# Rotary attention and a SiLU feed-forward on one core: a 128-row step in the products with v, the weights' sign on ScalarE, and a rewritten issue table

## The chip, the core and the metric

The kernel runs on one core of a Trainium2 chip. The metric is the device time of one execution in microseconds (us). The core's engines are TensorE (PE; its weight loads are listed as PEld), VectorE (DVE), ScalarE (ACT), GpSimd (POOL) and SyncE (SP), which here only issues DMAs. Each engine works its own instructions in the order in which they were issued and meets the others at semaphores.

## The reference

```python
# batch 4, heads 8, sequence 576, head size 64; model 512, d_ff 2048
q_rot, k_rot = rotate(q), rotate(k)                 # rotary embedding, halves of 32
scores = q_rot @ k_rot.T / sqrt(64)
attn = exp(scores - max(scores)); attn = attn / (sum(attn) + 1e-9)
x = (attn @ v).transpose(0, 2, 1, 3).reshape(2304, 512)
h = x @ w_in
return (h / (1 + exp(-h))) @ w_out                  # w_in, w_out arrive as float64
```

## The kernel before

Every float32 operand of a product is carried as two float16 parts, hi and lo, with a power-of-two scale that is taken from a norm of the data on the chip. A product is hi\*hi + hi\*lo + lo\*hi, summed in PSUM. Tokens of a batch are numbered in nine blocks of 64.

The work is cut into some 2,700 parts, each with the engines it may run on. The table `ORDER` lists part numbers with a letter for the engine (t TensorE, d VectorE, D VectorE with the sign change fused into the maximum, a ScalarE, p GpSimd, s and A the DMA queues of SP and ACT); a loop at the end issues them in that order. Nothing else sets the order on an engine.

- Attention: 144 slots. A slot has one score product `s` (L798), a row maximum (`max`: fused, L814, or plain, L819, which then needs a separate `neg`), `exp` on ScalarE (L830), a reciprocal of the row sum (`nr0`, `nr1`), then the split of the normalised row: `hi` through `part_hi` (L329 on VectorE or GpSimd, L335 on ScalarE) and `lo` through `part_lo` (one instruction on VectorE, L341; two on GpSimd, L329 and L344). A DMA transpose puts the two halves into `pt`. There are three `e` buffers, three `pn` buffers and two score buffers in PSUM.
- Products with v (`fpv`, L896): 32 groups (8 units by 4 head pairs). Each group has 14 steps over the 9 blocks of `pt`, and each step is two matmuls, one for each head of the pair, into the two halves of the PSUM partitions. In one of the 14 steps (the low part of v, block 4) only 64 of the 128 rows are used.
- Feed-forward: steps of 256 tokens by 256 of d_ff, `m1` (L950), tanh, `g` (L966), again a split `gh`, `gl`, and `m2` (L1006). Unit 0 is streamed while weights arrive; a last unit `rem` holds the remainders of all batches.
- Weights: the float64 bits of 8 pieces of w_in and w_out become float32 in four passes, `wT` (L659), `wC` (L666), `wS` (the sign bit, L675) and `wX` (L683), then a norm, then the split. They come in 12 whole places (1024 values a partition) and 8 half places (512).
- q, k and v: rope in three passes (L479, L483, L486), norms, splits (`qhi`, `qlo`, `vhi`, `vlo`).

Of the kernel before, what the change touches and what calls it, by code (L numbers as in the profile page):

```python
# [9 lines left out]
F16 = mybir.dt.float16  # L10
# [12 lines left out]
# Where the raw weights of a piece's two matrices are put (whole, or two halves): a, b, c are the  # L23
# ring's parts, i / o and a number the split weights' space of a piece that is written later.
# [19 lines left out]
765D 105d 559d 86a 758a 109t 143d 572s 759d 760d 136d 766a 92a 47d 767a 144d 117p 773t 774d 145d 61A 87d 137a
782t 768a 570d 48d 88s 108d 761a 769d 783D 563a 770a 784a 110d 775d 591s 564a 146d 138d 762d 785a 776a 565d 71d
93d 566d 573a 571d 574a 575d 771d 577t 560a 576d 561d 791t 123p 786a 787d 579t 111t 580d 112d 763s 593a 777a
592a 778d 596s 578d 792D 793a 788a 581t 582d 583d 772s 794a 795a 113d 800t 744d 613s 114d 796d 118p 584d 119d
598a 585a 139d 94s 801D 802a 95A 809t 810D 789d 594d 147s 811a 790s 645s 779a 780d 120a 781s 121d 618s 124p 125p
126a 587a 797a 798d 799s 803a 804a 595d 588d 818t 819D 115d 820a 812a 615a 813a 814d 805d 836t 837D 586d 127d
597a 821a 845t 599d 806a 838d 807d 646a 635s 156p 614a 122s 815a 816d 808s 589a 839a 817s 616d 840a 647a 600d  # L50
162p 841d 827t 822a 823d 620a 116d 824a 828D 829d 830a 831a 846d 825d 617d 648d 590d 847a 848a 649d 619a 636a
637a 621d 854t 855d 128s 849d 842p 832d 129A 2051t 638d 843d 856a 833a 834d 149a 826s 2052d 857a 858d 148a 2053d
157p 859d 850d 851a 872t 873D 863t 150t 864D 865d 844s 151d 866a 640s 2054t 163p 152d 164d 860a 874a 852d 639d
867a 835s 875a 641a 861d 868d 642a 890t 891D 643p 881t 882D 869a 892a 893a 883a 870d 894a 876a 853s 603t 2055a
862s 895d 622d 644d 884a 871s 601t 625t 896a 623t 604d 602d 605t 2056d 877d 885a 154d 606d 878a 626d 886d 607d
624d 887a 608d 611a 153d 650t 178s 651d 609a 879d 880s 888d 165a 652t 653d 612d 897p 2057t 2058a 654t 610d 655d
627t 628d 656d 917t 629d 155d 657d 158p 662a 2059d 630d 918D 919a 899t 900D 901d 660a 658p 166d 659d 920a 921a
902a 898s 908t 922d 903a 909d 631a 904d 935t 936d 923a 924d 663d 910a 889s 905a 686s 193p 937a 632d 911a 912a
2060t 2061a 938a 939a 925s 913d 2062d 926t 927d 944t 945D 946d 914a 664s 688a 928a 906d 907s 633p 634d 2147t
687a 915d 929a 2148a 947a 669s 930a 666a 745d 2149d 2150a 159p 948a 160d 689d 953t 661d 665a 940d 2151d 962t  # L60
# [146 lines left out]
def rope_attention_silu_ffn(  # L207
# [23 lines left out]
    B, H, S, D = q.shape  # L231
# [3 lines left out]
    NR = S // 64  # L235
# [135 lines left out]
    place = {}  # L371
# [737 lines left out]
```

## Time and profile before

| | |
|---|---|
| device time, median of 3 runs | 690.22 us (688.02 to 692.25) |
| span of the profiled execution, first to last instruction | 687.2 us |
| median minus that span | 3.0 us |
| busy share PE / DVE / ACT / POOL | 85% / 79% / 60% / 38% |
| instructions on DVE / ACT / POOL | 1222 / 852 / 217 |

The page lists one profiled execution, of which it gives the span. What lies around the span is the difference to the runs, 0.8 to 5.0 us. Busy time is the union of an engine's instructions. PE is pipelined, so its matmuls overlap, and how densely they are streamed is read from the distance between starts.

### The profile page before, as it was taken

What the parts mean: (1) busy time and instruction counts of PE and PEld (TensorE: products, weight loads), DVE (VectorE), ACT (ScalarE), POOL (GpSimd) and SP (SyncE); (2) the same over time, 40 slices, a digit from 0 to 9 for tenths busy, and PEclk for the clock granted to TensorE, in tenths of its full rate; (3) what the DMA queues carried; (4) which work ended last, traced back from release to release, by engine and by line L of the source; (5) the groups of instructions that cost most, each with busy time, mean ns of one, the idle gap of its engine ahead of it and who ended that gap; (6) DMA issues with size and microseconds to landing.
All of it is one profiled execution on the core that took longest, in us unless ns stands there. A gap on an engine that the chain in (4) does not pass through costs nothing.

```text
span 687.2 us, 12512 instructions
## 1 busy us (share of the span) xinstructions
PE 587.4 (85%) x4428; PEld 375.3 (55%) x4428; DVE 545.2 (79%) x1222; ACT 410.3 (60%) x852; POOL 257.7 (38%) x217
## 2 busy tenths in 40 slices
PE   3534376888799989998699899999999999999997
PEld 2412154645456555655366556656666665666664
DVE  5999989998999899989988989989868787312222
ACT  2488767978797666765455667566765544221421
POOL 1350344224455445342426436344163646022020
PEclk9955567989899999999899999999999999999999
DMA  9999995979699958989567779977964575410201
GB/s 259 236 242 233 275 168 124 237 155 219 128 162 161 188 96 168 173 165 178 97 135 157 135 127 192 164 137 134 197 118 71 104 128 94 54 31 1 47 1 31
DMA packets 233326, 98.33 MB, mean 143 GB/s; under 512 B 214192, under 2 KB 214448, under 8 KB 233264
## 3 DMA queue, kind: packets, MB, share of 16 engines
q1 hardware_dynamic: 232144, 95.47, 70.3%
q10 hardware_dynamic: 1120, 2.07, 1.5%
q8 instruction: 35, 0.57, 0.4%
q14 instruction: 27, 0.22, 0.1%
HBM read 36.16 MB, written 4.72 MB: 59 GB/s over the span
## 4 chain that ended last, share of the span: by engine, by line
PE 42%; DVE 25%; DMA 16%; ACT 7%; issue 6%; SPq 3%; POOL 1%; ACTq 0%; DVEq 0%; POOLq 0%
PE m L1006 15%; PE m L950 15%; DVE pn L341 6%; DMA pt<-pn 6%; PE pv L896 5%; DVE s L814 4%; PE s L798 3%; DMA w_in<-in_moe_w_in_dram 2%; DVE g L966 2%; DMA io<-in_k_dram 2%; ACT e L830 2%; PE s L354 2%; DMA io<-in_v_dram 2%; DVE vl L341 2%; DMA w_out<-in_v_dram 1%
## 5 line engine op out<-in xcount | busy, mean ns | idle before, releaser
L950 PEld LDWEIGHTS <-w_in 128*128 128x128 f16 x1728 | 167.0, 98 | 35.3 <-issue 5.4
L950 PE MATMUL m<-xh,w_in 128*128 128x256 f16 x1024 | 178.7, 273 | 3.1 <-DVE g L966 3.1
L1006 PE MATMUL m<-w_out,gh 128*128 128x512 f16 x576 | 172.4, 381 | 0.9 <-DVE ob L1019 0.6
L830 ACT ACTIVATE e<-s,small 128x576 f32<-128x576 f32 x144 | 109.7, 762 | 53.4 <-DVE s L814 22.4
L950 PE MATMUL m<-xl,w_in 128*128 128x256 f16 x512 | 139.7, 273 | 0.0
L341 DVE SCALAR_TENSOR_TENSOR pn<-e,small,pn 128x576 f16<-128x576 f32 x123 | 120.3, 986 | 10.9 <-ACT pn L335 5.4
L798 PE MATMUL s<-Tk,Tq 128*128 128x512 f16 (+1 forms) x512 | 90.7, 309 | 36.2 <-ACT e L830 26.8
L1006 PE MATMUL m<-w_out,gl 128*128 128x512 f16 x288 | 109.7, 381 | 2.2 <-DVE gl L341 2.2
L966 DVE SCALAR_TENSOR_TENSOR g<-g,m 128x512 f32<-128x512 f32 x72 | 49.0, 681 | 68.9 <-ACT g L962 43.8
L335 ACT ACTIVATE pn<-e,small 128x576 f16<-128x576 f32 x84 | 64.1, 768 | 45.2 <-DVE small L844 25.6
L814 DVE TENSOR_SCALAR_CACHE_REDUCE s<-s,small 128x576 f32<-128x576 f32 x101 | 81.7, 815 | 9.6 <-PE s L798 9.5
L798 PEld LDWEIGHTS <-Tq 128*128 128x128 f16 x512 | 41.3, 105 | 76.6 <-issue 41.0
L1006 PEld LDWEIGHTS <-gh 128*128 128x128 f16 x576 | 52.4, 100 | 55.5 <-issue 5.5
L962 ACT ACTIVATE g<-m,small 128x512 f32<-128x512 f32 x64 | 43.6, 682 | 61.3 <-PE m L950 56.7
L896 PE MATMUL pv<-pt,vh 128*64 128x256 f16 (+1 forms) x576 | 69.6, 308 | 3.9 <-DMA pt<-pn 1.7
L329 POOL TENSOR_SCALAR pn<-e,small 128x576 f16<-128x576 f32 x39 | 36.7, 941 | 91.2 <-DVE small L844 40.8
L341 DVE SCALAR_TENSOR_TENSOR gl<-g,small,gh 128x512 f16<-128x512 f32 x57 | 47.8, 839 | 10.5 <-ACT gh L335 6.6
L479 POOL TENSOR_TENSOR rt<-io,sin_t 128x576 f32<-128x576 f32 x21 | 32.3, 1547 | 45.8 <-DMA io<-in_k_dram 36.9
L1006 PEld LDWEIGHTS <-gl 128*128 128x128 f16 x288 | 28.2, 98 | 38.7 <-DVE gl L341 5.1
L896 PE MATMUL pv<-pt,vl 128*64 128x256 f16 (+3 forms) x320 | 47.7, 314 | 0.0
L896 PEld LDWEIGHTS <-vh 128*64 128x64 f16 x576 | 34.0, 116 | 20.5 <-issue 10.5
L335 ACT ACTIVATE gh<-g,small 128x512 f16<-128x512 f32 x43 | 30.8, 716 | 15.5 <-DVE g L966 15.2
(144 smaller groups left out, 879.3 us busy)
## 6 DMA issues: line engine op xcount, KB each, us to landing
out_dram<-ob SPq DMA_DIRECT2D x36, 128.0 KB, 2.4
w_in<-in_moe_w_in_dram SPq DMA_DIRECT2D x4, 1024.0 KB, 7.4
w_out<-in_moe_w_out_dram SPq DMA_DIRECT2D x4, 1024.0 KB, 7.3
io<-in_v_dram SPq DMA_DIRECT2D x13, 288.0 KB, 3.9
io<-in_q_dram SPq DMA_DIRECT2D x13, 288.0 KB, 3.3
io<-in_k_dram SPq DMA_DIRECT2D x13, 288.0 KB, 3.7
io<-in_v_dram SPq DMA_DIRECT2D x13, 256.0 KB, 4.5
ring<-in_moe_w_in_dram SPq DMA_DIRECT2D x3, 1024.0 KB, 6.0
```

The lines of the kernel that those rows point to most:

```text
L329: e.tensor_scalar(out=out, in0=in0, scalar1=s1, scalar2=s2, op0=ALU.mult, op1=ALU.bypass if s2 is None else ALU.mult)
L335: act.activation(hi, src, AF.Copy, scale=s)
L341: dve.scalar_tensor_tensor(out=lo, in0=src, scalar=s, in1=hi, op0=ALU.mult, op1=ALU.subtract)
L479: eng[e].tensor_tensor(out=buf("rt", b, p, nm), in0=x4()[:, :, ::-1, :], in1=sin_t, op=ALU.mult)
L798: pe.matmul(o, tq[:, j, 2 * c:2 * c + 2, :], kt[:, r0:r1, js], start=(n == 0), stop=(n == 1))
L814: dve.tensor_scalar(out=t, in0=t, scalar1=cc[:, 1:2], scalar2=None, op0=ALU.mult, op1=ALU.min, accum_out=m_of(1, 2),)
L830: act.activation(buf("e", i), buf("s", i)[:, 0:S], AF.Exp, bias=m_of(1, 2), scale=-1.0 if fused[i] else cc[:, 0:1], accum_out=m_of(2, 3),)
L896: pe.matmul(o[64 * j:64 * j + 64, 0:m], vt[part][0:k, j, s, :], pt[0:k, a, j, 0:m], start=(z == 0), stop=(z == len(steps) - 1),)
L950: pe.matmul(t[:, c, 0:n], w[:, wz, kk, fs], xx[:, kk, 0:n], start=(kk == 0 and x == 0), stop=(kk == KD - 1 and x == 2),)
L962: act.activation(g[:, :, 0:n], t[:, :, 0:n], AF.Tanh, scale=th_v[units[u][0]][:, i:i + 1])
L966: dve.scalar_tensor_tensor(out=g, in0=g, scalar=1.0, in1=t, op0=ALU.add, op1=ALU.mult)
L1006: pe.matmul(o, gs[gz][:, c, ts], w[:, wz, c], start=(first and c == 0 and x == 0), stop=(last and c == 1 and x == 2),)
```

## The change

It has three pieces.

1. In `fpv` every step uses all 128 rows. In the one step that used 64, the other 64 rows hold the low part of the first block on both sides, so the product gains one lo\*lo term.
2. `wS` may run on ScalarE, as one activation that writes float16.
3. `ORDER` is another table: the same 2,691 parts, in another order, and many of them on other engines. RAW_PLACE, GROUPS, the buffers and all other functions are as they were.

```diff
@@ fS
-                    if se == "d":
+                    if se == "a":
+                        act.activation(tu[:, :, 1].bitcast(F16), tf[:, :, 1], AF.Copy, scale=2.0 ** 30)
+                    elif se == "d":
                         dve.tensor_scalar(
                             out=tu[:, :, 1], in0=tu[:, :, 3], scalar1=0x8000, scalar2=None, op0=ALU.bitwise_and
                         )
...
-                n3 = add("wS", key, "dp", fS, [n1, n2], tb, it)
+                n3 = add("wS", key, "adp", fS, [n1, n2], tb, it)
@@ fpv
             for z, (a, part, s) in enumerate(steps):
-                k = 64 if part == "l" and a == 4 else 128
                 for j in range(2):
                     pe.matmul(
-                        o[64 * j:64 * j + 64, 0:m], vt[part][0:k, j, s, :], pt[0:k, a, j, 0:m],
+                        o[64 * j:64 * j + 64, 0:m], vt[part][:, j, s, :], pt[:, a, j, 0:m],
                         start=(z == 0), stop=(z == len(steps) - 1),
                     )
@@ ORDER
-4s 0d 5t 3s 1s 6d 21d 15d 7t 2s 38s 41t 22d 23d 8d 39t 42d 16p 540s 40d 9t 10d 11d 62s 12d 24a 13d 63t 43t 17d
...
```

What the new table does to the engines, counted from the built programs (instructions by line, before and after):

| | VectorE | ScalarE | GpSimd |
|---|---|---|---|
| lo halves (`lo` 22, `qlo` 4, `gl` 4 move) | 258 to 228 (L341) | | 42 to 72 (L344) |
| hi halves of rows and of g (`hi`, `gh`) | 39 to 30 | 127 to 103 | 50 to 83 |
| sign of weights | 19 to 1 | 0 to 19 | 1 to 0 |
| row maximum, fused / plain | 101 / 43 to 84 / 60 | | |
| rope passes | 33 to 49 | | 63 to 47 |
| v hi, x hi, outputs | 16 to 27 | 52 to 39 | 2 to 4 |
| `wT` and `wC` | 0 to 4 | 40 to 34 | 0 to 2 |
| `neg` and `nr0` instructions | 64 to 77 | 123 to 127 | |

Three of the 16 `ksw` parts (two DMAs each) also go from the ACT queue to the SP queue. On TensorE the parts stand almost as they did: counted in TensorE work, the first `m1` and each unit's steps stand where they stood.

VectorE near its start, before. `w_in` and `w_out` are here both the first weight piece (128x1024) and q and k of batch 0 (128x576), which lie in the same space; L479, L483 and L486 are rope passes, L358 reads a norm from PSUM:

```order
L675 TENSOR_SCALAR w_in<-w_in 128x1024
L358 SCALAR_TENSOR_TENSOR junk_128,small<-m_188,id_t 128x128
L486 TENSOR_TENSOR w_out<-w_out,rt 128x576
L310 TENSOR_SCALAR small<-m_160 128x2
L483 TENSOR_TENSOR w_out<-w_out,cos_t 128x576
L329 TENSOR_SCALAR small<-small 128x1
L310 TENSOR_SCALAR small<-m_188 128x1
L486 TENSOR_TENSOR w_out<-w_out,rt 128x576
L316 TENSOR_SCALAR small<-small 128x1
L683 SCALAR_TENSOR_TENSOR w_in<-w_in 128x1024
L341 SCALAR_TENSOR_TENSOR n<-w_in,small,n 128x9x64
L675 TENSOR_SCALAR w_out<-w_out 128x1024
```

VectorE at the same place now (`wX` is L686 in the new file):

```order
L358 SCALAR_TENSOR_TENSOR junk_128,small<-m_204,id_t 128x128
L310 TENSOR_SCALAR small<-m_169 128x2
L316 TENSOR_SCALAR small<-small 128x2
L686 SCALAR_TENSOR_TENSOR w_in<-w_in 128x1024
L329 TENSOR_SCALAR small<-small 128x1
L341 SCALAR_TENSOR_TENSOR n<-w_in,small,n 128x9x64
L358 SCALAR_TENSOR_TENSOR junk_127,small<-m_227,id_t 128x128
L341 SCALAR_TENSOR_TENSOR n<-w_in,small,n 128x9x64
L310 TENSOR_SCALAR small<-m_227 128x1
L486 TENSOR_TENSOR w_out<-w_out,rt 128x576
L316 TENSOR_SCALAR small<-small 128x1
L686 SCALAR_TENSOR_TENSOR w_out<-w_out 128x1024
```

The two sign passes are gone from VectorE. They stand on ScalarE, whose first rows were these before:

```order
L335 ACT_TABLE_LOAD
L335 ACTIVATE n<-w_in,small 128x9x64
L659 ACTIVATE w_in<-w_in 128x1024
L666 ACTIVATE w_in<-w_in 128x1024
L659 ACTIVATE w_out<-w_out 128x1024
L335 ACTIVATE n<-w_in,small 128x9x64
L666 ACTIVATE w_out<-w_out 128x1024
```

ScalarE's first rows now (L676 is the new sign pass):

```order
L659 ACT_TABLE_LOAD
L659 ACTIVATE w_in<-w_in 128x1024
L666 ACTIVATE w_in<-w_in 128x1024
L676 ACTIVATE w_in<-w_in 128x1024
L335 ACTIVATE n<-w_in,small 128x9x64
L659 ACTIVATE w_out<-w_out 128x1024
L666 ACTIVATE w_out<-w_out 128x1024
L676 ACTIVATE w_out<-w_out 128x1024
```

Each weight place now has three passes in a row on ScalarE, and one of the two early q and k halves (`n`) has left it.

GpSimd between the score products of slots 108 and 114, before (`n`, `io` and `rt` belong to q and k of the last batch, `pn` and `e` to attention slots, `gh` to the feed-forward):

```order
L329 TENSOR_SCALAR n<-io,small 128x9x64
L486 TENSOR_TENSOR io<-io,rt 128x576
L329 TENSOR_SCALAR pn<-e,small 128x576
L329 TENSOR_SCALAR gh<-g,small 128x512
L329 TENSOR_SCALAR pn<-e,small 128x576
L329 TENSOR_SCALAR e<-e,small 128x576
L344 TENSOR_TENSOR pn<-e,pn 128x576
L479 TENSOR_TENSOR rt<-io,sin_t 128x576
L483 TENSOR_TENSOR io<-io,cos_t 128x576
L486 TENSOR_TENSOR io<-io,rt 128x576
```

GpSimd between the same two products now:

```order
L329 TENSOR_SCALAR pn<-e,small 128x576
L329 TENSOR_SCALAR gh<-g,small 128x512
L329 TENSOR_SCALAR g<-g,small 128x512
L344 TENSOR_TENSOR gl<-g,gh 128x512
L329 TENSOR_SCALAR gh<-g,small 128x512
L329 TENSOR_SCALAR pn<-e,small 128x576 x2
L479 TENSOR_TENSOR rt<-io,sin_t 128x576
L329 TENSOR_SCALAR pn<-e,small 128x576
L486 TENSOR_TENSOR io<-io,rt 128x576 x2
```

Rope passes have left GpSimd, and halves of slots and of the feed-forward have come in their place.

## Rows read from the trace of the kernel before

**Rows 1.** The page: the span, then busy time, share and instructions of each engine.

```profile
span 687.2 us, 12512 instructions
PE 587.4 (85%) x4428; PEld 375.3 (55%) x4428; DVE 545.2 (79%) x1222; ACT 410.3 (60%) x852; POOL 257.7 (38%) x217
```

**Rows 2.** Busy time by stage: window, length, PE, PEld, DVE, ACT, POOL, clock, DMA.

```profile
20.00:160.00 140.00, 87.01 (x594) 55.91 (x595) 132.77 (x298) 107.38 (x192) 48.98 (x30) 0.72 0.97 207
160.00:500.00 340.00, 313.03 (x2432) 197.36 (x2431) 308.95 (x691) 225.85 (x492) 148.63 (x123) 0.98 0.82 155
500.00:600.00 100.00, 99.00 (x814) 63.41 (x813) 69.47 (x172) 49.71 (x114) 43.78 (x45) 1.00 0.55 95
600.00:687.00 87.00, 82.24 (x559) 54.39 (x556) 20.94 (x32) 22.87 (x52) 14.34 (x16) 1.00 0.10 22
```

**Rows 3.** Groups by form on VectorE: busy us, mean ns of one, idle before.

```profile
L341 DVE SCALAR_TENSOR_TENSOR pn<-e,small,pn 128x576 f16<-128x576 f32 x123 | 120.3, 986 | 10.9 <-ACT pn L335 5.4 <-POOL pn L329 3.6 <-POOL g L329 0.9
L814 DVE TENSOR_SCALAR_CACHE_REDUCE s<-s,small 128x576 f32<-128x576 f32 x101 | 81.7, 815 | 9.6 <-PE s L798 9.5
L819 DVE TENSOR_REDUCE small<-s 128x1 f32<-128x576 f32 x43 | 32.1, 748 | 2.0 <-PE s L798 1.7 <-PE s L804 0.2
L341 DVE SCALAR_TENSOR_TENSOR vl<-io,small,vh 128x320 f16<-128x320 f32 x26 | 20.3, 797 | 3.5 <-ACT vh L335 2.8 <-POOL vh L329 0.7
L814 DVE DVE_READ_ACCUMULATOR s<-s,small 128x1 f32 x101 | 14.1, 139 | 0.0
L329 DVE TENSOR_SCALAR pn<-e,small 128x576 f16<-128x576 f32 x21 | 13.0, 618 | 2.9 <-DMA pt<-pn 2.3 <-DVE small L844 0.4
L483 DVE TENSOR_TENSOR io<-io,cos_t 128x576 f32<-128x576 f32 x7 | 7.6, 1085 | 0.7 <-ACT n L454 0.6
L675 DVE TENSOR_SCALAR w_out<-w_out 128x1024 uint16<-128x1024 uint16 x4 | 5.3, 1325 | 0.2 <-ACT w_out L666 0.2
L675 DVE TENSOR_SCALAR w_in<-w_in 128x512 uint16<-128x512 uint16 x3 | 2.3, 754 | 0.4 <-ACT w_in L659 0.4
```

**Rows 4.** Groups by form on GpSimd.

```profile
L329 POOL TENSOR_SCALAR pn<-e,small 128x576 f16<-128x576 f32 x39 | 36.7, 941 | 91.2 <-DVE small L844 40.8 <-DMA pt<-pn 13.0 <-DVE w_in L683 9.5
L483 POOL TENSOR_TENSOR io<-io,cos_t 128x576 f32<-128x576 f32 x19 | 32.3, 1711 | 20.2 <-ACT small L837 12.8 <-ACT n L454 4.8 <-issue 1.8
L344 POOL TENSOR_TENSOR pn<-e,pn 128x576 f16<-128x576 f32 x21 | 28.6, 1361 | 1.8
L329 POOL TENSOR_SCALAR e<-e,small 128x576 f32<-128x576 f32 x21 | 18.6, 886 | 46.5 <-ACT pn L335 24.7 <-DVE pn L329 11.3 <-ACT small L837 6.0
```

**Rows 5.** A weight pass on ScalarE, by form.

```profile
L659 ACT ACTIVATE w_in<-w_in 128x1024 f32<-128x1024 f32 x4 | 4.5, 1131 | 0.0
```

**Rows 6.** Timeline of VectorE and GpSimd, 206 to 230: start, us, instruction.

```profile
206.53 1.00 DVE L341 SCALAR_TENSOR_TENSOR vl<-io,small,vh 128x320 f16<-128x320 f32 x2
225.31 0.80 DVE L341 SCALAR_TENSOR_TENSOR pn<-e,small,pn 128x576 f16<-128x576 f32 x1
227.92 2.02 DVE L341 SCALAR_TENSOR_TENSOR vl<-io,small,vh 128x320 f16<-128x320 f32 x2
...
227.54 1.59 POOL L344 TENSOR_TENSOR pn<-e,pn 128x576 f16<-128x576 f32 x1
```

**Rows 7.** Timeline of TensorE inside one product with v.

```profile
311.91 0.33 PE L896 MATMUL pv<-pt,vl 128*64 128x320 f16 x2
312.05 0.33 PE L896 MATMUL pv<-pt,vh 128*64 128x320 f16 x2
312.31 0.32 PE L896 MATMUL pv<-pt,vl 64*64 64x320 f16 x2
312.56 0.73 PE L896 MATMUL pv<-pt,vh 128*64 128x320 f16 x8
```

**Rows 8.** The products with v alone by stage: busy TensorE, clock, DMA.

```profile
500.00:687.00 187.00, 18.01 (x228) 1.00 0.34 61
```

**Rows 9.** Shares of the chain that ended last, 0 to 130.

```profile
by line: DMA w_in<-in_moe_w_in_dram 9.5%; DMA io<-in_v_dram 8.0%; DMA w_out<-in_v_dram 7.9%; issue 7.2%; DMA io<-in_k_dram 6.2%; SPq L509 5.5%; PE pv L896 4.8%; DMA Tq<-w_out 4.5%; DVE pn L341 4.0%; PE s L354 4.0%; DVE s L814 3.7%; DMA io<-
```

More of the change, by code (lines that the diff above doesn't have):

```diff
@@ L44 @@
[L44 to L48, printed above, removed]
@@ new lines @@
+1108d 203d 185d 204d 205d 186d 1095d 206a 2072t 2203d 223s 1109a 207d 2204p 208d 242a 1124t 217d 1110d 231s
+2073a 1116D 1125D 1117a 1118a 249p 2205t 2074d 1126d 1101d 1111d 230s 747d 241a 2211t 250p 1112a 1096s 251p
+2206d 1102d 1113d 2208t 2212a 1103a 2213d 1133t 1119a 255d 2214a 243t 2218t 1104d 1127a 2215d 232a 1105s 244d
+1128d 245d 1134d 1114s 246d 1142t 256d 2219a 2216t 252a 247d 2209d 257p 1135a 1120d 2220d 2217t 1129d 253d 2221a
+258p 1136a 2225t 254s 2222p 259d 1121a 1143d 262s 1122d 1144a 1137a 1151t 2226a 1130p 233t 1138d 1152d 1145a
@@ new lines @@
+368a 2335d 369d 2336t 370d 2339a 1419d 394a 409s 2340d 1448t 2337t 1469a 2341d 1420s 1449d 2342p 1436a 402t
+1450d 1451a 2345t 385s 403d 1452a 1470a 1471d 418p 1437d 1411s 404t 2346a 1472p 2343t 405d 411a 1473p 395t 410a
+2344t 396d 406d 1453d 2347d 1484t 2348a 424p 1474s 1457t 2352t 1458d 1454p 1438s 397d 1459a 1485D 1455p 2349d
+1486a 1487a 412t 2353a 1493t 413d 398d 1488d 407d 1460a 2350t 2354d 1456s 414d 1494D 1461a 2355p 392A 1475t
+1462d 425d 1495d 2351t 1463p 1496a 408d 2356d 1497a 399p 1502t 1489d 416d 1490a 2359t 1464d 415d 1503D 1465s
@@ new lines @@
+1880t 1866d 2500t 1881d 1861s 1872d 1882a 1883a 2496d 1867d 1873a 2497d 1868p 1884a 1898t 2501a 2492t 1899D
+1874a 1869d 2498t 1885d 531d 1870s 1886a 2128d 1900a 1901a 1875d 1907t 1876d 2502d 1877p 2129t 1887d 2503a 1878p
+1908d 1889t 1888s 2130d 1909a 2499t 1910a 1890D 2504p 2131d 1879s 1891a 1892a 1902d 1916t 1911d 1903d 1912d
+2132t 1893a 1917d 1918a 1904p 1925t 1913p 2133d 2505t 2134d 1894d 1905d 1926d 2511t 1906s 1919a 1895d 1896p
+2508t 2512a 1914p 1897s 2513d 1943t 2514a 2518t 1944D 1920d 1927d 1945a 1946a 1915s 2506d 1928a 2515d 1921d
@@ new lines @@
+1947a 1952t 1922d 2519a 1979t 1923p 2509a 2520d 2516t 1929a 1930d 1980D 1931a 2525t 1981d 2521p 1924s 1982a
+2522d 1948d 1953D 1949p 1988t 1954a 2526a 1950d 2517t 1932d 1951s 1955a 1983d 1989d 2523t 1956a 1984d 1957d
+1933s 2527d 1958p 1934t 1990d 1991a 2135t 1935D 2528a 1959d 1936d 1985p 2529d 1937a 1960s 1961t 1986p 1992a
+2524t 1938d 1939d 1962D 1993d 1994d 2532t 1987s 1995p 2024t 2533a 1940p 1996s 2530t 1963a 1964a 2534d 1941p
+1965a 2535a 2042t 1966d 2025D 2539t 2536d 2026d 2027a 1942s 1967a 2043D 1968p 2507s 1970t 2540a 2531t 1971D
@@ new lines @@
+2136a 2541d 1969s 1972a 1973a 2537t 2044d 2542p 1974a 2045a 1975d 2028d 2137d 2543p 2546t 1976a 2029d 2046d
+2047d 1977d 2030d 1978s 2006t 2547a 2031p 1997t 2007d 2048a 2138t 1998D 2008d 1999d 2548d 2000a 2009a 2538t
+2032s 2001d 2049d 2002d 754d 2003a 2139d 2015t 2549p 2050s 2544t 2140d 2016D 2033t 2010d 2004d 2017a 2018a 2553t
+2011d 2034d 2012a 2005s 2550d 2035d 2019d 2036a 2020d 2545t 2554a 2021p 2037d 2013d 2551t 2038d 2555d 2014s
+2022d 2552t 2556d 2023s 2557d 2141t 2039d 2040d 2041s 2560t 2142d 2143d 2558t 2561a 2562d 2144t 2563d 2564d
@@ new lines @@
+2559t 2145d 2146d 2565t 2571t 2568t 2572a 2573d 2569a 2566d 2578t 2574p 2570s 2575d 2510s 2576t 2579a 2450s
+2580d 2577t 2567s 2581a 2582d 2585t 2583t 2586a 2587d 2584t 2588a 2589d 2592t 2590t 2593a 2594d 2591t 2595a
+2596d 2599t 2597t 2600a 2601d 2602d 2606t 2603d 2598t 2607a 2608d 2604t 2609a 2610d 2613t 2605t 2614a 2615d
+2611t 2616d 2617d 2620t 2612t 2621a 2622d 2618t 2623d 2624p 2631t 2619t 2632a 2625t 2633d 2634d 2638t 2626d
+2635p 2627s 2636t 2639a 2628t 2640d 2645t 2641p 2629d 2642p 2630s 2637t 2646a 2643t 2647d 2648d 2652t 2649d
@@ L175 @@
+2644t 2653a 2650t 2654d 2655d 2659t 2656p 2651t 2660a 2657t 2661d 2662a 2666t 2663p 2658t 2667a 2664t 2668d
+2669d 2673t 2670p 2665t 2674a 2671t 2675d 2676p 2680t 2677p 2672t 2681a 2678t 2682d 2683p 2679t 2684d 2685t
 2688t 2686d 2687s 2689a 2690s
```

234 lines of the change are left out of this document (104 added, 130 removed).

## The prediction

> **What bounds the kernel now.** I read the page's totals first, then busy time by stage, then the groups, then single stretches. The totals [rows 1] name no engine: TensorE is busy for 85% of the span, VectorE for 79%. The stages do [rows 2]. From 20 to 160 us VectorE is busy for 132.77 of 140 us (95%) and TensorE for 87.01; from 160 to 500 us VectorE for 308.95 of 340 (91%), with TensorE at 313.03. From 500 us on VectorE falls to 69% and then 24%, and TensorE stands at 99% and 95%. The reader is to see two kernels: 480 us in which VectorE has next to no idle time left, and 187 us of matmuls. TensorE's own share in the first part is no proof of a bound, since its matmuls overlap in the account and it waits in between. So an edit is worth something ahead of 500 us if it takes time from VectorE, and behind that only if it takes time from TensorE. ScalarE, at 107 of 140 and 226 of 340 us, and GpSimd, at 49 and 149 us, have room. The start has a second limit: up to 160 us the DMA engines stand at a share of 0.97 [rows 2], and the five largest DMA pieces of the chain that ended last make up 36% of it up to 130 us [rows 9].
>
> **What leaves VectorE.** Thirty lo halves go (22 of attention rows, 4 of q and k, 4 of the feed-forward). At 986 ns [rows 3] that is 29.6 us. Nine hi halves go, at 618 ns: 5.6. Of the sign passes 11 whole ones at 1.325 us and 7 halves at 0.754 go: 19.9. Seventeen row maxima turn from fused (815 + 139 ns) to plain (748): 17 x 0.206 = 3.5. Together 58.6 us.
>
> **What comes to it.** Sixteen rope passes. The nearest row is 1.085 us for L483, a mean that holds two blocked ones; a plain pass of this width costs what the plain maximum does, 0.75. Bounds 12.0 and 17.4; I take the middle, 14.7. Eleven scalings of outputs, x and v and four weight conversions are wide: 15 at 0.75 or more, 11.3. Thirteen one-column instructions come at the 139 ns of the accumulator read, 1.8. Together 27.8. VectorE's net is -30.8 us, out of 545.
>
> **What this does to the others.** GpSimd takes 30 lo halves of two instructions each (886 + 1361 ns [rows 4]): 67.4; 33 hi halves at 941 ns: 31.1; two v halves of twice that width: 3.8; one pass more on weights: about 1.3; and it loses 16 rope passes at 1.711: -27.4. Net +76 us, on 257.7. ScalarE gains 19 sign passes, whole ones at the 1.131 us of its other weight pass [rows 5], halves at half that: 17, and loses 24 hi halves, 13 scalings and 6 weight passes, which is more than it gains. Neither becomes the bound by its sum: GpSimd would be near half of the span. What an in-order queue of that load does to a slot is a rival below.
>
> **What GpSimd costs VectorE.** A clean lo half takes 0.80 us and two clean halves of v 1.00 [rows 6]. The means are 0.986 for 123 of the first and 0.797 for 26 of the second [rows 3]. So 123 x 0.186 + 26 x 0.297 = 30.6 us of VectorE's time in these two groups is no work. A stretch shows what it is [rows 6]: the two v halves at 227.92 take 2.02 us, and GpSimd's subtraction had begun at 227.54 and ran until 229.13. Spread over GpSimd's 257.7 us this is 0.12 us lost for each us of GpSimd. Groups that I left out (the lo halves of g, q, k and the weights) lose some too, so I take 0.2. The ends: 0, if the new instructions stand beside row maxima, whose mean of 815 ns the trace shows undisturbed; and 1.02 lost for 1.59, which is 0.64, if each stands as the one in rows 6. At 0.2 the added 76 us cost 15 us (0 to 49).
>
> The Trainium skill, SBUF — State Buffer, Who interferes with whom, has a rule that speaks against this part: VectorE instructions with two SBUF inputs and GpSimd instructions that read SBUF exclude each other through a shared port, and whichever starts second stands for the whole of the first. Rows 6 agree: of GpSimd's 1.59 us there were 1.21 left when the v halves started, and 1.02 were lost. The rule gives no rate; that depends on who meets whom.
>
> **The start.** Counted by the order, 16 of the 30.8 us lie ahead of the first `m1`: 7 whole and 3 half sign passes (11.5), six lo halves (5.9), less small ones. This is where the chain shows DMA. I let a quarter of it go to that: 4 us lost (0 to 16).
>
> **The 128-row step.** The pairs of matmuls start 0.14 us apart [rows 7]. The pair of 64 rows starts 0.26 us behind the one before it, and the next 0.25 us behind it: 0.51 where 0.28 would do, 0.23 us in each of 32 groups, 7.4 us of TensorE time. Behind 500 us stand 228 matmuls of these products [rows 8], that is 8 groups of 28, in the stage where TensorE is full: 1.9 us are real. Of the other 24 (5.5 us) the cover is VectorE's queue; a quarter counts: 1.4. Together 3.3 us (1.9 to 7.4). If the cover goes, since VectorE gets shorter, more of it counts, so the two pieces help each other.
>
> The Trainium skill, TensorE: Matmul & The Clock Gate, table "Why this matters for your kernels", says that a matmul over fewer rows takes the time of one over 128. By that alone this piece would be worth 0 and the forecast would be 678. The row differs: 0.26 and 0.25 against 0.14. It is the change of shape between neighbours that costs here.
>
> **Queues.** Three `ksw` parts go from ScalarE's DMA queue to SP's. They are short on both, and SP stands between transposes and their halves anyway: nothing, unless a later transpose waits behind a `ksw` whose own transpose has not landed. The order on TensorE is the old one but for neighbours, and the tail behind the last product with v is the same work: nothing. ScalarE's first sign passes stand ahead of a q half; VectorE's own lo halves wait for that, and this is in the 4 us of the start.
>
> **The sum.** -30.8 + 15 + 4 - 3.3 = -15.1 us. The first three are VectorE's, in a stretch where it is busy for 91 to 95%, so I count them whole. The profiled execution would go from 687.2 to 672.1 us. The median of the runs is 3.0 us above that span; with it, 675 us.
>
> **Rivals.**
> *More of it.* GpSimd costs only the 0.12 that the two groups show (9 us), the start loses nothing, and TensorE gets most of its 7.4 us: -30.8 + 9 - 5.5 = -27, 663 us. For it: VectorE is as full in the start as later. Against it: the DMA pieces. With no cost of GpSimd at all it would be 652.
> *No difference: the start is DMA's.* If all 16 us ahead of the first `m1` are absorbed by loads, VectorE's sum is -30.8 + 16 + 15 = 0, and 3.3 us of TensorE remain: 687 us. For it speaks rows 9; against it that VectorE is busy for 95% there.
> *Slower: GpSimd takes the port.* The place is 160 to 500 us, where most of the added halves stand: its lo half is two instructions, 2.25 us, beside a VectorE that mostly works on splits of the same kind. At a rate of 0.4 VectorE's gain is gone, from 0.54 on the kernel is slower by over 1%, and at the 0.64 of rows 6 VectorE has 18 us more than before: 15 us slower, 705. The three `pn` buffers press the same way, since a slot split on GpSimd holds its buffer for 2.25 us where VectorE needs 0.80. For it: the skill's rule on the shared port, and that the added instructions are of the exposed kind. Against it: the mean rate over 217 GpSimd instructions is a third of 0.64 or less.
> *It doesn't do what it says* can be left out for the sign and the step: they are counted in the program.
>
> **Chances.** Forecast (668 to 683) 0.45, more of it 0.17, no difference 0.20, slower 0.18. About 1% is what a measurement of this kernel can tell from no change: faster than 683.3 us 0.60, within 0.22, slower than 697.1 us 0.18. For 8 in 10 the range goes from 655 (a part of the case without any cost of GpSimd is left out) to 699 (the upper half of the slower case is left out). The likeliest case's own range is 668 to 683.
>
> **What would show it.** Right: VectorE's busy time near 530 us (545.2 - 30.8 + 15) and GpSimd's near 335; the mean of the lo half on VectorE at 1.0 to 1.1 us; no pair of matmuls in the products with v more than 0.14 us behind the one before; the first `g` earlier than before by some 10 us, and the stretch in which TensorE stands at 99% beginning near 487 us. The step on GpSimd is wrong if the lo half's mean is above 1.2 us, or if VectorE shows new idle time behind GpSimd's `pn`. The step on the start is wrong if the first `g` comes no earlier though the sign is gone. What would make the prediction wrong altogether is a wait that no sum shows: a slot whose halves stand in GpSimd's queue behind a rope pass, so that the transpose, the product with v and the unit behind it come late while VectorE has nothing to do.

## The result and the profile after

The changed kernel takes 667.93 us (median of 4 runs, 665.7 to 668.9); the kernel before took 689.8 us beside it. The ratio is 0.9643, with a 95% interval of 0.9612 to 0.9674: 24.6 us of 690, or 21.9 us between the medians. The profiled execution took 668.9 us with a span of 667.1, against a span of 687.2. It is the slowest of the four, whose spans go from 663.9 to 667.1 us, so a difference between two single spans is uncertain by a few us.

The page of the changed kernel: span, then busy time, share and instructions of each engine, the answer to [rows 1].

```profile
span 667.1 us, 12566 instructions
PE 580.9 (87%) x4428; PEld 380.2 (57%) x4428; DVE 523.1 (78%) x1195; ACT 415.0 (62%) x829; POOL 335.3 (50%) x297
```

VectorE has lost 22.1 us, GpSimd has gained 77.6. Busy time by stage in the windows of [rows 2], changed kernel (the last one is shorter, since the kernel ends at 667):

```profile
20.00:160.00 140.00, 84.10 (x565) 55.31 (x566) 120.68 (x278) 116.99 (x184) 67.75 (x52) 0.88 0.84 197
160.00:500.00 340.00, 328.02 (x2608) 213.26 (x2607) 307.52 (x712) 234.25 (x514) 209.81 (x183) 0.98 0.85 162
500.00:600.00 100.00, 99.80 (x802) 66.04 (x801) 65.50 (x151) 42.38 (x90) 35.27 (x38) 1.00 0.53 88
600.00:667.00 67.00, 62.15 (x418) 40.69 (x416) 17.59 (x27) 13.56 (x39) 14.99 (x17) 1.00 0.07 17
```

Fixed windows hold different work in the two kernels. So I cut both at the same work: the first `g`, and the starts of the 14th, 24th and 32nd product with v. Before, with PE, PEld, DVE, ACT and POOL in that order:

```profile
0.00:125.00 125.00, 63.31 (x421) 41.19 (x422) 112.26 (x266) 82.99 (x143) 38.49 (x27) 0.71 0.97 222
125.00:311.00 186.00, 167.55 (x1274) 105.28 (x1275) 172.91 (x386) 140.46 (x294) 82.39 (x64) 0.96 0.86 165
311.00:474.00 163.00, 149.36 (x1174) 94.15 (x1170) 147.90 (x320) 95.90 (x219) 72.47 (x61) 0.98 0.79 148
474.00:591.00 117.00, 115.90 (x938) 74.46 (x939) 88.56 (x218) 65.71 (x143) 50.03 (x51) 1.00 0.68 119
591.00:687.00 96.00, 91.23 (x628) 60.26 (x628) 23.55 (x36) 25.26 (x57) 14.34 (x16) 1.00 0.09 20
```

The changed kernel, cut at the same work:

```profile
0.00:128.00 128.00, 63.99 (x420) 42.16 (x421) 105.72 (x250) 96.69 (x145) 55.24 (x46) 0.91 0.88 222
128.00:308.00 180.00, 164.94 (x1251) 106.99 (x1251) 164.58 (x378) 140.10 (x280) 102.74 (x86) 0.93 0.84 162
308.00:457.00 149.00, 147.22 (x1194) 95.75 (x1191) 133.40 (x304) 96.99 (x222) 99.61 (x87) 1.00 0.86 164
457.00:572.00 115.00, 114.75 (x946) 75.74 (x944) 92.52 (x225) 61.61 (x136) 62.07 (x62) 1.00 0.69 123
572.00:667.00 95.00, 89.95 (x624) 59.53 (x622) 26.91 (x43) 19.62 (x47) 15.69 (x18) 1.00 0.10 23
```

The five stages changed by +3, -6, -14, -2 and -1 us. The two that shrank most are those in which VectorE lost 8.3 and 14.5 us. (How much of this the order makes and how much the engines is seen in the fourth kernel below.) In the third, TensorE's busy time fell by 2.1 us only, and the rest of the 14 is its idle time: 13.6 us before, 1.8 now. From 308 us on the kernel is a row of matmuls. The list of what TensorE waited for (total us, times, longest) says who had held it there. Before, 311 to 474 us:

```profile
PE pv L459 <- DVE x_rem L914: 5.7, 2, 4.4
PE s L798 <- ACT e L830: 2.3, 2, 1.2
PE m L1006 <- DVE gl L341: 2.2, 3, 1.0
PE m L950 <- DVE g L966: 1.6, 1, 1.6
```

The changed kernel, 308 to 457 us, the whole list:

```profile
PE s L801 <- ACT e L833: 1.2, 3, 0.5
PE pv L898 <- DMA pt<-pn: 0.5, 1, 0.5
```

The three waits for VectorE that are shown, 9.5 us together, are gone. Groups by form on VectorE, changed kernel, the answer to [rows 3] (L483 now has 16 passes where [rows 3] had 7):

```profile
L341 DVE SCALAR_TENSOR_TENSOR pn<-e,small,pn 128x576 f16<-128x576 f32 x101 | 97.5, 968 | 3.9 <-POOL pn L329 1.9 <-ACT pn L335 1.7
L817 DVE TENSOR_SCALAR_CACHE_REDUCE s<-s,small 128x576 f32<-128x576 f32 x84 | 68.0, 815 | 10.9 <-PE s L801 10.8
L341 DVE SCALAR_TENSOR_TENSOR gl<-g,small,gh 128x512 f16<-128x512 f32 x53 | 48.1, 908 | 5.7 <-ACT gh L335 3.2 <-POOL gh L329 2.1
L822 DVE TENSOR_REDUCE small<-s 128x1 f32<-128x576 f32 x60 | 44.8, 748 | 6.2 <-PE s L801 5.7 <-PE s L807 0.2
L341 DVE SCALAR_TENSOR_TENSOR vl<-io,small,vh 128x320 f16<-128x320 f32 x26 | 18.3, 719 | 0.2 <-ACT vh L335 0.2
L483 DVE TENSOR_TENSOR io<-io,cos_t 128x576 f32<-128x576 f32 x16 | 12.4, 778 | 0.0
```

The lo half of a row and the v half did not get dearer beside a busier GpSimd. They got cheaper: 986 to 968 ns, 797 to 719. The lo half of `g` did get dearer, from 839 to 908 ns; its row before was:

```profile
L341 DVE SCALAR_TENSOR_TENSOR gl<-g,small,gh 128x512 f16<-128x512 f32 x57 | 47.8, 839 | 10.5 <-ACT gh L335 6.6 <-POOL gh L329 3.3
```

GpSimd's groups, the answer to [rows 4], and ScalarE's weight pass beside its new sign pass, the answer to [rows 5]:

```profile
L329 POOL TENSOR_SCALAR pn<-e,small 128x576 f16<-128x576 f32 x61 | 60.1, 987 | 82.2 <-DVE small L847 38.8 <-DMA pt<-pn 12.4 <-DVE small L310 10.5
L344 POOL TENSOR_TENSOR pn<-e,pn 128x576 f16<-128x576 f32 x43 | 59.4, 1382 | 3.6
L329 POOL TENSOR_SCALAR e<-e,small 128x576 f32<-128x576 f32 x43 | 43.0, 1000 | 30.8 <-ACT pn L335 14.8 <-DVE pn L329 9.2 <-ACT small L840 3.4
...
L659 ACT ACTIVATE w_out<-w_out 128x1024 f32<-128x1024 f32 x4 | 4.6, 1142 | 1.4 <-DMA w_out<-in_moe_w_out_dram 1.4
L676 ACT ACTIVATE w_out<-w_out 128x1024 f16<-128x1024 f32 x4 | 10.0, 2498 | 0.1
L676 ACT ACTIVATE ring<-ring 128x512 f16<-128x512 f32 x4 | 5.4, 1354 | 0.5 <-DVE ring L329 0.5
```

The sign pass costs ScalarE 2.50 us where its neighbour of the same width costs 1.14. And the products with v run through all their steps (one of them in the timeline of TensorE, changed kernel, the answer to [rows 7]):

```profile
309.27 0.30 PE L898 MATMUL pv<-pt,vl 128*64 128x320 f16 x2
309.41 0.30 PE L898 MATMUL pv<-pt,vh 128*64 128x320 f16 x2
309.55 0.30 PE L898 MATMUL pv<-pt,vl 128*64 128x320 f16 x2
309.68 0.71 PE L898 MATMUL pv<-pt,vh 128*64 128x320 f16 x8
```

### The profile page after: what moved, and what is told of

It reads as the page before. It is cut to its first block, busy times and chain, and to the rows that moved or that the text cites. A ratio compares the mean times of both kernels' runs of the same rounds, so it can differ in the third digit from the quotient of the medians.

```text
span 667.1 us, 12566 instructions
## 1 busy us (share of the span) xinstructions
PE 580.9 (87%) x4428; PEld 380.2 (57%) x4428; DVE 523.1 (78%) x1195; ACT 415.0 (62%) x829; POOL 335.3 (50%) x297
## 4 chain that ended last, share of the span: by engine, by line
PE 53%; DVE 12%; issue 3%; DMA 2%; ACT 2%; POOL 1%; SPq 0%; DVEq 0%; POOLq 0%; ACTq 0%
PE m L952 21%; PE m L1008 20%; PE s L801 5%; PE pv L898 5%; DVE pn L341 3%; DVE s L817 2%; DVE g L968 1%; PE s L807 1%; DVE small L329 1%; DVE small L822 1%; DMA Tk<-Tk 1%; DVE vl L341 1%; DMA pt<-pn 1%; DMA io<-in_v_dram 1%; ACT g L964 1%
## 5 line engine op out<-in xcount | busy, mean ns | idle before, releaser
L952 PE MATMUL m<-xh,w_in 128*128 128x256 f16 x1024 | 181.3, 275 | 4.8 <-DVE g L968 4.7
L801 PE MATMUL s<-Tk,Tq 128*128 128x512 f16 (+1 forms) x512 | 91.8, 309 | 44.4 <-ACT e L833 31.1
L329 POOL TENSOR_SCALAR pn<-e,small 128x576 f16<-128x576 f32 x61 | 60.1, 987 | 82.2 <-DVE small L847 38.8
L341 DVE SCALAR_TENSOR_TENSOR pn<-e,small,pn 128x576 f16<-128x576 f32 x101 | 97.5, 968 | 3.9 <-POOL pn L329 1.9
L801 PEld LDWEIGHTS <-Tq 128*128 128x128 f16 x512 | 41.9, 105 | 85.8 <-issue 49.7
L817 DVE TENSOR_SCALAR_CACHE_REDUCE s<-s,small 128x576 f32<-128x576 f32 x84 | 68.0, 815 | 10.9 <-PE s L801 10.8
L898 PE MATMUL pv<-pt,vh 128*64 128x256 f16 (+1 forms) x576 | 66.3, 304 | 0.8 <-DMA pt<-pn 0.5
L344 POOL TENSOR_TENSOR pn<-e,pn 128x576 f16<-128x576 f32 x43 | 59.4, 1382 | 3.6
L335 ACT ACTIVATE pn<-e,small 128x576 f16<-128x576 f32 x70 | 53.5, 767 | 10.8 <-DVE small L847 8.1
L329 POOL TENSOR_SCALAR e<-e,small 128x576 f32<-128x576 f32 x43 | 43.0, 1000 | 30.8 <-ACT pn L335 14.8
L341 DVE SCALAR_TENSOR_TENSOR gl<-g,small,gh 128x512 f16<-128x512 f32 x53 | 48.1, 908 | 5.7 <-ACT gh L335 3.2
L822 DVE TENSOR_REDUCE small<-s 128x1 f32<-128x576 f32 x60 | 44.8, 748 | 6.2 <-PE s L801 5.7
L329 POOL TENSOR_SCALAR g<-g,small 128x512 f32<-128x512 f32 x19 | 15.0, 789 | 61.2 <-DVE gh L329 57.2
```

Of the source, the lines that this page charges most:

```text
L329: e.tensor_scalar(out=out, in0=in0, scalar1=s1, scalar2=s2, op0=ALU.mult, op1=ALU.bypass if s2 is None else ALU.mult)
L335: act.activation(hi, src, AF.Copy, scale=s)
L341: dve.scalar_tensor_tensor(out=lo, in0=src, scalar=s, in1=hi, op0=ALU.mult, op1=ALU.subtract)
L344: e.tensor_tensor(out=lo, in0=src, in1=hi, op=ALU.subtract)
L801: pe.matmul(o, tq[:, j, 2 * c:2 * c + 2, :], kt[:, r0:r1, js], start=(n == 0), stop=(n == 1))
L817: dve.tensor_scalar(out=t, in0=t, scalar1=cc[:, 1:2], scalar2=None, op0=ALU.mult, op1=ALU.min, accum_out=m_of(1, 2),)
```

## The experiments

My theory after the result: VectorE's queue set the stages from 128 to 457 us, and the parts that left it are the gain. The rivals were that the step or the order made the gain, and that the start was never VectorE's. Lines in kernels with a shorter table lie some 40 lower than in the changed kernel (L301 for L341, L761 for L801).

**The step alone**, both ways. The first kernel is the one before with the edit, the second is the changed one without it.

```diff
-                k = 64 if part == "l" and a == 4 else 128
```

> The kernel before with the 128-row step alone. If VectorE covers TensorE up to 500 us, as the prediction has it, the step gives 3.3 us: ratio to before 0.995. If TensorE is the one waited for wherever a product with v stands, it gives its whole 7.4 us: ratio 0.989. If rows cost nothing by themselves: 1.000.

> The changed kernel with the 64-row step put back. TensorE is at 98 to 100% from 250 us on there, so the theory of a TensorE bound expects the whole 7.4 us back: 675 us, ratio to before 0.979. The theory of a VectorE bound expects 3.3 us: 671 us, ratio 0.973. The pair of 64 rows should start 0.26 us behind its neighbour again.

Measured: the step alone 0.996 (0.9936 to 0.9985), that is -2.8 us; without it the changed kernel stands at 0.9695 (0.9664 to 0.9726), 3.6 us (±3) above 0.9643. In the timeline of TensorE of the changed kernel without the step, the gap is back:

```profile
309.24 0.30 PE L859 MATMUL pv<-pt,vh 128*64 128x320 f16 x2
309.47 0.32 PE L859 MATMUL pv<-pt,vl 64*64 64x320 f16 x2
309.72 0.73 PE L859 MATMUL pv<-pt,vh 128*64 128x320 f16 x8
```

0.23 and 0.25 us against 0.14. The step is worth about 3 us in either kernel, neither 0 nor 7.4.

**Order and engines apart.** The third kernel has the old order with the new engine letters, the fourth the new order with the old letters; both have the 128-row step. 474 letters differ, of which the first are these (old order, old and new letters):

```diff
-17d 49d 55d 543d 18a 548d 84d 91p 117p 774d 61A 570d
+17p 49p 55p 543a 18p 548a 84p 91d 117d 774D 61s 570a
```

> The old issue order, with each part on the engine that the new table gives it, and the 128-row step. If the sums of work on VectorE carry the gain, this is as fast as the changed kernel but for a few us: 668 to 673 us. If the gain needs the places too (halves on GpSimd beside VectorE's reads of PSUM, early enough for their slots), it is 683 us or more, and the mean of the lo half on VectorE rises above 1.05 us.

> The new issue order, with each part on its old engine (the sign on VectorE), and the 128-row step. If the engines carry the gain, only the step is left: 682 to 687 us. If the order alone carries it, it is near 670 us. If order and engines were made for each other, it is slower than before: over 690 us.

Measured: new engines in the old order 1.0667 (1.0624 to 1.0709), 738.01 us; new order with the old engines 1.0033 (1.0006 to 1.0059), 695.36 us. Against the step alone the one loses 49 us and the other 5; together they win 22 (0.996 to 0.9643). Seen from the new order, the order alone costs 5.0 us and all the engine moves on top of it win 26.9 (1.0033 to 0.9643). With the step's 2.8 that is the whole 24.6.

The stages of the fourth kernel, cut at the same work (first `g` at 131.2 us; with the step alone it came at 122.9):

```profile
0.00:131.00 131.00, 65.14 (x420) 42.77 (x421) 115.04 (x262) 82.65 (x143) 34.67 (x27) 0.91 0.89 214
131.00:320.00 189.00, 167.03 (x1256) 108.22 (x1257) 171.05 (x386) 137.87 (x292) 82.36 (x63) 0.93 0.81 157
320.00:475.00 155.00, 148.00 (x1194) 95.38 (x1192) 142.32 (x321) 93.38 (x217) 70.61 (x60) 1.00 0.81 155
475.00:598.50 123.50, 116.58 (x945) 75.95 (x941) 92.16 (x221) 67.14 (x148) 49.29 (x51) 1.00 0.62 115
```

Against the step alone (122.9, 188.7, 163.4, 116.2 and 96 us) the order by itself makes the start 8 us longer, the third stage 8 shorter and the fourth 7 longer. The engine moves then take 3, 8, 6, 9 and 1 us off the five stages. These are single executions; before and step alone, which have the same work up to the first `g`, are 1.8 us apart there.

The new engines in the old order do all that the sums ask: VectorE is busy for 530.7 us, GpSimd for 326.3. What they lose is seen in VectorE's waits (third kernel, whole span):

```profile
DVE pn L301 <- ACT pn L295: 22.0, 14, 4.4
DVE small L807 <- ACT small L800: 12.9, 17, 2.7
DVE pn L301 <- POOL pn L289: 12.9, 9, 4.9
DVE gl L301 <- POOL gh L289: 12.8, 6, 4.6
```

In [rows 3] the lo half waited 5.4 us for ScalarE's hi half, and 3.6 for GpSimd's; in the changed kernel it is 1.7 and 1.9. So in the old order a hi half that has gone to another queue lands too late, and VectorE stands at the lo half behind it.

**One part back at a time**, in the changed order: the 19 sign passes to VectorE (one of them to GpSimd), the 28 attention lo halves that had moved to GpSimd back to VectorE, and the ropes back (25 passes from VectorE to GpSimd, 9 the other way). The first letters of each, in this order:

```diff
-543a 548a 570a 575a 648a 594a
+543d 548d 570d 575d 648d 594d
...
-762p 843p 870p 915p 951p 960p
+762d 843d 870d 915d 951d 960d
...
-17p 49p 55p 84p 91d 117d 118d 124d
+17d 49d 55d 84d 91p 117p 118p 124p
```

> The changed kernel with 19 sign passes on VectorE (18) and GpSimd (1) again, in their new places; they come to 19 us of VectorE time ahead of 185 us, 11 of them ahead of the first g. If VectorE bounds the start, the kernel takes 10 to 19 us more: 678 to 687. If loads, the slots' own chain or ScalarE's queue bound it, less than 5 us more; if ScalarE does, the first g even comes earlier than 128 us.

> The changed kernel with 28 lo halves of attention rows (3 ahead of the first g, 11 more up to 310 us, 11 up to 457 us) on VectorE again, in their new places: 28 x 0.81 = 22.7 us more for VectorE, 28 x 2.38 = 67 less for GpSimd. If VectorE bounds the middle and GpSimd costs it little: 15 to 22 us slower, 683 to 690. If GpSimd's halves cost VectorE 0.2 us for each of theirs (13 us), only 5 to 9 us slower: 673 to 677. If the middle is TensorE's: no change.

> The changed kernel with the rope passes on their old engines, in their new places (25 passes go from VectorE to GpSimd, 9 the other way). GpSimd took 76 us more work and yet the mean of the lo half on VectorE fell from 986 to 968 ns. If it is the rope passes (two inputs, 1.4 to 1.7 us each) that block VectorE, this mean rises to 1.0 us or more and the clean 12 us that VectorE gets back are largely lost. If composition does not matter, the mean stays at 0.97 and VectorE's busy time falls by 12 us. The time itself can get worse by waits of k and q for GpSimd: 670 to 690.

Measured, with the difference to 0.9643 in us of 690 (each ±3 us, from the half widths of the two intervals as squares), the difference of the two profiled spans, and that of the mean spans of all runs:

| put back | ratio (95%) | by ratio | by profiled span | by mean span | VectorE busy | GpSimd busy |
|---|---|---|---|---|---|---|
| sign | 0.977 (0.9733 to 0.9807) | +8.8 | +5.1 | +8.0 | +19.4 | +10.3 |
| lo halves | 0.9725 (0.9692 to 0.9758) | +5.7 | +4.6 | +4.7 | +9.2 | -67.3 |
| ropes | 0.9805 (0.9768 to 0.9841) | +11.2 | +10.5 | +10.7 | +2.2 | +19.8 |

The profiled span is low for the sign because that execution was the fastest of its four; the ratio and the mean span agree. The three parts add up to 25.7 us by ratio, against 26.9 for all the engine moves in this order. So in this order the parts' prices nearly add, and the moves that were not tested alone (hi halves, maxima, scalings) make no more than the uncertainty together.

The lo halves give the rate. 28 at 0.80 us would bring VectorE 22.4 us; it got 9.2, so 67.3 us less on GpSimd gave 13.2 back: 0.20 us for each. The ropes give another: sixteen passes net left VectorE, 12.0 us at 0.75, and it got busier by 2.2. So 19.8 us more on GpSimd took 14.2: 0.7 for each. The groups by form of the kernel with the ropes put back show where:

```profile
L301 DVE SCALAR_TENSOR_TENSOR pn<-e,small,pn 128x576 f16<-128x576 f32 x101 | 105.4, 1046 | 5.6 <-POOL pn L289 3.0 <-ACT pn L295 2.3
L301 DVE SCALAR_TENSOR_TENSOR gl<-g,small,gh 128x512 f16<-128x512 f32 x53 | 51.9, 980 | 5.7 <-ACT gh L295 3.2 <-POOL gh L289 2.1
```

968 and 908 ns have become 1046 and 980. That is 7.9 + 3.8 of the 14.2 us. Its third stage is 154 us long instead of 149, though VectorE is busy for 134 there as in the changed kernel: most of the 11 us is not VectorE's work, which grew by 2.2. What holds that stage is not shown; TensorE's longest listed wait there is 4.1 us for `e`.

The same traces allow a second count, instruction by instruction: the time of each VectorE instruction above what its form needs undisturbed (the tenth percentile over ten of these traces), put down to the GpSimd instruction that it overlaps most. The excess was 72 us before and is 74 now, while the undisturbed work fell by 27. Of it, what fell on instructions beside a rope pass on GpSimd went from 44 to 20 us, with 105 and then 71 us of rope passes there; what fell beside the two instructions of a lo half went from 11 to 27 us, with 89 and then 163 us of these. So per us of GpSimd the rope passes cost 0.42 before and 0.28 now, the halves 0.12 and 0.17: the kind matters, and so does the place.

**The sign on ScalarE in the old order.** The kernel with the step alone, and the 19 sign passes on ScalarE.

```diff
-543d 548d 570d 575d 594d 599d
+543a 548a 570a 575a 594a 599a
```

> The kernel before with the 128-row step and the same 19 signs on ScalarE, all else in the old order. Against the step alone (0.996 of before): if VectorE bounds the start, 8 to 16 us less, 671 to 679; if it doesn't, within 4 us of 687; if ScalarE's queue is what the exponentials of the start stand in, slower, 690 or more.

Measured: 1.0217 (1.0162 to 1.0272), 707.5 us, some 18 us slower than the step alone, though VectorE is busy for 17.2 us less. Its first `g` comes at 133.7 us instead of 122.9. Ahead of it the lo halves of rows on VectorE wait 11.5 us for ScalarE's hi halves, and with the step alone less than 1. The part that is worth some 9 us in the new order costs 18 in the old one, and 18 of the 49 us that the new engines lose there come with it alone.

**Who sets the start.** First 2 MB more are loaded ahead of the third pair of q and k (copied to a place that nothing reads); then VectorE gets an idle pass of the same width beside each sign pass of ScalarE (its result is not read).

```diff
+            if b == 0 and p == 2:
+                for z in range(4):
+                    sp.dma_start(out=extra[128 * z:128 * z + 128], in_=w_out[128 * z:128 * z + 128])
...
+                        dve.reduce_max(
+                            out=junk[0][:, 0:2].bitcast(F32),
+                            in_=ones[:, None, :].to_broadcast([128, 4 * nh, 128]), axis=AX.XY,
+                        )
```

> The changed kernel with 2 MB of loads that nobody reads, from DRAM to DRAM, queued ahead of the third pair of q and k. In the first 20 us the DMA engines moved 286 GB/s, so 2 MB are about 7 us of them. If loads bound the start, the first g comes 5 to 10 us later (133 to 138 us) and the kernel takes 4 to 9 us more. If not, both move by less than 2 us.

> The changed kernel with 19 idle passes on VectorE, one beside each sign pass on ScalarE: each reads a constant in SBUF as wide as the pass it replaces (about 1.1 us whole, 0.6 half), 17 us together, ScalarE unchanged. If VectorE bounds the start and the weights' stage behind it, 12 to 17 us slower (680 to 685). If it has slack there, under 5 us. Against the run with the sign back on VectorE (7 us slower than the changed kernel), the difference is what the sign passes cost on ScalarE: if they cost something, this run is the slower one by that.

Measured: with more loads 0.9737 (0.9703 to 0.977), with idle passes 0.9708 (0.9671 to 0.9746). The stages of the kernel with more loads:

```profile
0.00:134.00 134.00, 65.00 (x420) 42.94 (x421) 103.79 (x250) 96.73 (x145) 54.55 (x46) 0.90 0.89 226
134.00:314.00 180.00, 164.29 (x1258) 106.52 (x1259) 164.94 (x378) 140.71 (x282) 104.27 (x86) 0.94 0.86 164
```

The first stage is 6 us longer, the second as long as without the loads, and the span is 5 us longer (6.5 by ratio): what the start loses to a load is not given back. The idle passes (18.7 us of work) lengthened VectorE's busy time by 11.8 us and the kernel by 4.5 by ratio (5.6 by profiled span), less than half. The sign back on VectorE costs 8.8 for 19.4 us, a like share. So a cost of the sign's place on ScalarE, which would make this run the dearer one, is not seen in the new order; the two runs do not load VectorE by the same amount, and the test is no finer than that.

**Two tries at a better kernel.** Nine more rope passes from GpSimd to VectorE; and the four lo halves ahead of the first `g` back to VectorE.

```diff
-17p 49p 55p 84p 164p 455p 456p 480p 513p
+17d 49d 55d 84d 164d 455d 456d 480d 513d
...
-762p 843p 870p 915p
+762d 843d 870d 915d
```

> The changed kernel with nine rope passes moved from GpSimd to VectorE (those that were there before). If a rope pass on GpSimd costs VectorE about 0.5 us for each of its own, as the run with 16 more of them on GpSimd says, VectorE pays 9 x 0.75 = 6.8 us and gets back 9 x 1.5 x 0.5 = 6.8: its busy time stays at 523 us, GpSimd's falls by 13, and k and q come earlier: 664 to 669 us. If a rope pass costs only the 0.2 of a lo half, VectorE has 4 us more and the kernel takes 670 to 672.

> The changed kernel with the four attention lo halves that stand ahead of the first g, and had moved to GpSimd, back on VectorE (4 x 0.80 us = 3.2 us more for VectorE, 4 x 2.3 = 9 us less for GpSimd there). With all 28 lo halves put back the first g came at 125.9 us and not at 128.0. If the start is set by what GpSimd and ScalarE queue ahead of it and what is won there is kept, the first g comes at about 126 again and the time falls by 2 us, to 666 (ratio 0.961). If the start's gain is given back to VectorE in the stage behind it, as 4 of the 5 us of the earlier run suggest, the first g comes earlier and the 14th product with v does not: 668 to 671 (0.964 to 0.969). If loads alone set the start, the first g stays at 128 and the time at 668 to 670.

Measured: the first 0.9707 (0.9665 to 0.9749), at the edge of the intervals slower than the changed kernel, against the expectation. Nine passes came to VectorE, and its busy time went from 523.1 to 522.7, so 13.5 us less on GpSimd gave back the 6.8 that they cost, and 0.4 more: 0.5 for each. But in the profiled execution the first `g` came at 131.0 us, 3 later, and the span was 4.2 longer: a gain in busy time, a loss in place. The second: 666.64 us, ratio 0.9655 (0.9616 to 0.9694), which can't be told from 0.9643. In its profiled execution, the fastest of its six, the first `g` came at 123.6 us, and the span is 663.1 us. So there, too, the difference of the start passed to the end (4.4 and 4.0 us); but the median doesn't bear out that the edit made it.

## Why the prediction came out as it did

The forecast was 675 us, 15 below before; measured were 22 to 25 below, inside the range and at the fast edge of the likeliest case's own. The mechanism (time taken from VectorE shortens the kernel until TensorE fills) held in its direction. The places did not, and two errors met. Of the signs that I had named, GpSimd's busy time (335) came true; the lo half's mean (0.968 us, not 1.0 to 1.1), VectorE's busy time (523, not 530), the first `g` and the start of TensorE's full stretch did not.

**What bounds the kernel.** VectorE was the bound from 125 to 474 us in so far as these stages shrank by 20 us while it lost 22.8 us of work there, and TensorE's waits for it went away. But I counted its time whole, and pieces put back one at a time don't cost that: by ratio the sign 8.8 of 19.4 us, the lo halves 5.7 of 9.2, the idle passes 4.5 of 11.8. The ropes cost 11.2 us for 2.2 of VectorE. So the near equality of 20 and 22.8 is partly luck: the sign and the lo halves gave less than VectorE's time and the ropes more, and 8 of the 14 us in the third stage are there with the order alone, in which VectorE's busy time hardly falls (543.4 us in all, 547.1 with the step alone). I also did not read the ceiling. TensorE had 13.6 us of idle time in the third stage, and when these were used up VectorE counted for little; with the lo halves put back VectorE has 3.9 us more there, and the stage is 1 us longer. I expected TensorE's full stretch from 487 us, and it begins at 308.

**What leaves and what comes to VectorE.** The counts of -30.8 held, two prices did not. I priced the lo halves that leave at their disturbed mean of 986 ns; at the clean 0.80 of [rows 6] thirty of them are 24.0 us, 5.6 less. A rope pass costs 0.75 us undisturbed (0.78 on the mean at L483 now), not the middle of 0.92 that I took: 2.7 us less. Together that is -27.9, and the count by instruction shows -27.

**What GpSimd costs VectorE.** This step failed in its kind. I spread one rate over all of GpSimd's time and then took 0.2 for the net +76 us. The rate of 0.2 is right for lo halves (13.2 of 67.3). But the 27.4 us of rope passes that leave GpSimd cost VectorE 0.5 to 0.7 each, not 0.2. By the count by instruction the excess rose by 2 us, where I had put 15: the rope passes gave back about what the halves and the other additions took. So the rope part, which I had booked as a cost (14.7 on VectorE, less 5.5 given back by GpSimd), is a gain of about 11 us, the largest of the four in its middle value, though not clear of the sign's within ±3. Contention explains why VectorE is busy for no less with the ropes back on GpSimd; VectorE's time explains only 2.2 of the 11 us, and the cause of the rest stays open. The rival in which GpSimd takes the port had the right mechanism and the wrong instruction: at 0.7 for everything it would have come true.

The Trainium skill, SBUF — State Buffer, Who interferes with whom, bears on this: two-input work on VectorE and GpSimd instructions that read SBUF exclude each other. The runs agree in so far as VectorE lost time beside GpSimd, by 13 us and by 14; put back one at a time, a rope pass costs some three times what a half costs for each us on GpSimd.

**The start.** I let 4 of 16 us go to DMA. All went, and 3 us more: the first `g` came at 128 us, not 10 earlier. 2 MB of extra loads moved it by 5.9 us, where the expectation had 7 us of DMA time for them, so the rival in which loads set the start has its mechanism shown. But loads are not the only setter, and the larger part of this error is the order: with the old engines in the new order the first `g` comes at 131.2 us, 8 later than with the step alone, and the engine moves win 3 of these back. ScalarE's queue carries 13.7 us more there, and TensorE's waits for `e` from ScalarE are longer, but that is not what sets the start in this order: with the sign back on VectorE ScalarE is busy for 21 us less there, the waits are longer still and the first `g` comes at 130.9 us. The waits before (0 to 125 us), in the changed kernel (0 to 128) and with the sign back (0 to 131):

```profile
PE s L798 <- ACT e L830: 20.5, 8, 6.5
...
PE s L801 <- ACT e L833: 27.7, 13, 7.5
...
PE s L761 <- ACT e L793: 33.4, 16, 9.3
```

Beside this lies a mis-sized term: I priced the sign pass on ScalarE at 1.131 us, 17 us in all, and it took 2.50, and 1.35 for halves: 38 us. It showed in the old order, where the sign alone makes the first `g` 11 us later.

**The order.** "Nothing" was wrong as a step. The order alone costs 5 us, the engines alone 49, and only both together win. Which of its moves does it I have not taken apart; the waits of the third kernel suggest that it sets hi halves early enough for the queue that now makes them.

**The step.** 3.3 us forecast, 2.8 and 3.6 measured. The Trainium skill's table in TensorE: Matmul & The Clock Gate (Why this matters for your kernels), by which the rows of a matmul don't count, would have made it nothing; the traces don't agree where neighbours change their rows.

**Where the numbers met.** By place I had -12 us for the start, about -1 from there to 474, and -2 behind. Measured were +3, -20 and -3. The start's error of 15 us (8 of it the order's) and the middle's of 19 (8 of it the order's too, the rest the engines') nearly cancelled. The total was closer than its working.

## What to carry to other kernels

Contention between two engines goes by the kind of instruction and by what it stands beside, not by busy time alone: find in the trace what a partner loses beside each kind, and price work that leaves at its undisturbed time. Look first at what leaves the shared place. A stage's gain ends where the next engine is full, so read ahead of the sum how much idle time that engine has in the stage. An edit of engines and its issue order are one edit: half of it can lose more than the whole wins. And compare parts that are put back in the new order with all of them put back in the new order, not with the kernel before.

## What the runs showed of the hardware

A rope pass on GpSimd (a product or sum of two float32 operands, 128 by 576, 1.44 to 1.71 us) cost VectorE 0.5 to 0.7 us for each us when such passes were put back or taken away, the two instructions of a lo half 0.2.

ScalarE's sign pass, which reads every second float32 and writes every fourth float16, took 2.50 us for 1,024 values a partition; its pass that reads the same and writes float32 in place took 1.14.

The mean granted clock of TensorE in the first 125 us, over stretches at its two levels of 1.2 and 2.4 GHz, was 0.71 before and 0.96 with the step alone, at the same span of 687.2 us; so it did not set the time here. TensorE is busy for about half of that stage.
